# One table replaced: the order of every engine's steps in a fused attention and gated feed-forward kernel

## The chip, the cores and the metric

The kernel runs on one core of a Trainium2 chip. The metric is device time in microseconds (us). The kernel before was timed in three runs: 216.54, 216.66 and 220.53 us, median 216.66. One further execution was recorded by the hardware profiler; its span, from the first to the last instruction, is 213.9 us at a granted TensorE clock of 1.000.

## What is computed

Block-sparse attention for 4 batches of 8 heads, 768 tokens and 64 channels, in blocks of 32 tokens (a row of blocks also sees three sampled ones). The heads' outputs are put side by side (512 channels) and go through a feed-forward layer whose gate is a convolution over three neighbouring tokens.

```python
scores = scale * np.matmul(q, k.transpose(0, 1, 3, 2))
mask = np.abs(blk_i - blk_j) <= window
mask = mask | (blk_i == 0) | (blk_j == 0) | (blk_i == n_blocks - 1) | (blk_j == n_blocks - 1)
...
scores = np.where(mask, scores, -1000000000.0)
attn = np.exp(scores)
attn = attn / (np.sum(attn, axis=-1, keepdims=True) + 1e-09)
return np.matmul(attn, v).astype(np.float32)
...
h = np.maximum(x @ w_in, 0.0)
for k in range(K):
    conv_out += conv_w[k][None, None, :] * hp[:, k:k + S, :]
gate = 1.0 / (1.0 + np.exp(-conv_out))
return (h * gate @ w_out).astype(np.float32)
```

## The kernel before

The program first builds a list of 1758 steps. Each step has a name, the engines that may do it, the steps it needs, and the buffers it takes. A table, ORDER, then says in which order the steps are put down. For each it holds two characters (the step's number to base 64), one letter for the engine where the step has a choice (P TensorE, A ScalarE, V VectorE, G GpSimd, S SyncE), and one character for each buffer that the step is the first to use. put_down reads the table and calls each step's function; that is all the scheduling there is. Every engine then runs its own steps strictly in that order, and waits where an input or a buffer is not ready.

The steps, in the order in which data goes through them:

- Loads. Sixteen pairs of heads (four for each batch) need q, k and v. The first pair comes in float32 by SP and ACT queues. All others are issued by POOL (L239), with conversion to bf16. POOL issues in order, and between the loads stand tiny "pace" copies (L414, L656) that make POOL wait until a given exp, or an earlier load, is done.
- Getting q and k transposed into a slot (tiles e and o, five slots). Pairs 0 to 5: TensorE transposes (L466 for k, L504 for q) into PSUM, copied on by DVE or ACT (L340, L336). Pairs 6 to 15: two DMA transposes issued by SP (L581, stg<-nat), then two DVE copies (L340, e<-stg and o<-stg). Rows 64 to 87 of a slot hold the mask; they are made once (L309, L320 and L322, k rows by L340 or L336) and copied to the other slots (24-row copies). v is copied into its tile beside a column of ones (v_cp: vt<-vn).
- 144 attention units, 18 for each half batch of 384 tokens ("segment"). The last half batch is cut into a segment of 256 and one of 128 tokens, so there are nine, 0 to 8. A unit is two steps of score matmuls on TensorE (L742, st<-e,o; 8 blocks of 128x128, 1024 columns), one exp on ACT (L753, pt<-st), and two steps of matmuls with v (L775, av<-vt,pt). Two PSUM buffers st, two av and two mix; six pt buffers. So the scores of unit u+2 wait for the exp of unit u.
- After the last av step of a pair of heads: reciprocal (L692, rcp) and normalisation (L694, xtok<-av,rcp) on DVE, then a transpose of xtok into xT. In segments 0, 1, 7 and 8 this is done by TensorE (L713) and a copy (x_cp). In segments 2 to 6 it is a DMA transpose issued by SP (L703, xT<-xtok), four for each segment.
- First feed-forward matmuls (L864, mix<-xT,winb), which need all four xT parts of their segment; relu by ACT (L884) or DVE (L886) into hE; three products and two sums for the convolution on DVE (L916, L924), or, for segment 8, matmuls with diagonal matrices (L935); tanh on ACT (L963, L940); plus one (L966) and product (L971, gT<-m,hE) on DVE.
- Second feed-forward matmuls (L802, mix or st<-woutb,gT), four steps of two for each of 24 blocks of 128 tokens; eviction ("ev", o2s<-mix) by ACT (L336) or DVE (L340); store issued by SP (L809).

SP's queue therefore carries, in table order, the L581 and L703 transposes, the stores, and eight small copies of mask rows for the last batch (m_last, o<-mlast and e<-mlast).

The engine is a choice of the table for these steps alone: the casts of the first pair, copies out of PSUM (k_cp, q_cp, x_cp), the two mask copies, v_cp, relu and ev. In the kernel before, DVE does 13 of 16 v_cp, 30 of 64 relu and 11 of 24 ev.

Of the kernel before, what the change touches and what calls it, by code (L numbers as in the profile page):

```python
# [25 lines left out]
6o15yV6p690Z6d6e6q05+16t04v1P05/V6i6j6u6k06y16l6v14w6z160+6m06r06s6A26nV6D00S6E0X4xhW12l06F3hZ00/6I16JhX4y2m6K4
h+hYV06R06Sh/Vi316T5i4ii06W14z176Xik6wi5Ai00iji16Y04A2x11Q1i2V6/0701RAil4B6x2116B7417111SV6C75iq1290im6G762ic1
2aV47d0idir7ein7i14C2bV2z26H7j7f36L6M1is2c04DieV6U6V6Z7k46+7n06N12eV7oit2217p5722dV7s17t24V2n023V7u0737x0iu7y2q1
2oV02B02A7z1777G16O7H784E2pV2F27g0iv7h7L07926P0io4F7l2H37M7I27a7m7q7rip07v7w7A7N37B16QV17Q12rV7R7J0W7K7b07S47V0
7C07W2kV47O2sV7X57D2C4G82183107P7E17T8407cV8707FV887Uiw7Y8918c1ix2J12I7Z8d2yV0i602GV18e28h04H7+12N08i7/i7i918j3  # L30
4Ii8V2f0ia8508m12DV1ibA8nif08o4igiy28u0iz868a8vihAiA2P8z12Q18A8w5iBiO1iG3800iP8B0iC8E02K4J2t18biH8f8FiDiI8J12S8g
8kiJ8l81A8K8piE8q18G18x8yiK2g08CiF8D2RiL8H2iViQ2hV2OA28IiMiU02EViV8L2iN2T0iW2LV2iR2X2Y18R0iSA08SiX8T38W1iYV18X
i+18Y4i/2MV8/090j0Vj109158r2941958sj22Uj71960j3V9909a8Mjm0j409b12+9h1jo2/08t29i8Njnj89j2j58O0jp9m09nj9V8U0j6A8V
319r1jq9o3ja1jbju1jd0jvjrje8P9s9w0jcAjx8Z321308+92jfA93jwjj19t49xjC2jg0jhjyiZ9y5369E1js372jkjiV9798jz9cjE9F2u0jD
9d19G09J0jA9k9KjF9l9L19e19O1jt9p9q339PjlV9u2wA9T02vAjB9U9vk819Q2jK3k9jL9z9V3jGjY0393a29Y19f9A9ZjHjMa409g9H09IjN
9M9+4jZjOa59N9R8QjI9SjP9W3c9XjJa91aaa65kajQiT9/jRj+3bab09B2ae09Cj/2VV3af9Dk0A2kb3h2WVaj1ag1k20a11a2k33d0kcA3k4
2ZA3k5jS1k6V1a30jT34V4akjUal2ar0k1jVa01asjWA0ke0kfat3jXkh1kgV1kiaw135V3kkjAax3l3kn0ay4kokC03i0kk1kEaB0kpAklkDaC
kmAa7kFa8acaG1aD5kq0kGadaHkK1kt1kH3nahkMaL0kr3o13mkLaI0aikuksVamaMkvAkNkz03eaN1aT1kOaUkw1kS2ankPkx3skIkAao0kTaY0
aV2aZkJ1au0avazaAkyVaEkBAaFaJb11kVa+3b2aKkQl61apaOb34b60kRaqb7lc0kUb85be1k+3bfl7l03pbg0aP1kWaWbj0bkaQ2aXk/kXa/b0
b4bo1aRb5b9bl1bal1aSbh0bpldkYl2bq2bt0bikZbubmbb1l3lebcby1bzbv3bdl4bnl8l5brbsbA43qV0bG0bHk7l938V43fV1bI5lf3v3w1  # L40
laV2bL1bMlgA0bwbQ03rVli1bN0lh3gVljll0kdlkV3jA0lm3AbRlblnVbV1bWbS1lr1lG0lo0lIlsbX23x3B1lplHc10c2ltV3t1lqAbxc61lJ
c33c7bBbC1lO1lx1lylKc84cb0bJlzVcclD0lLlQcg1bKlP3ychlu1cd5bD0lRbObPlvbEbTci0lElMcl0bF1lSbUcmlwAbY3KlNct13L0lTlA1
lW2bZculYcn1c40lB3zlXc5c9calFVcv33Hcy03I2czb+2lUcelZlCAmg03PlVcA4cD1cfcEl+mh3Mb/cF2cjcI0ck3uV1ma1c0m23l/cJcom3
cp1cQ1cRcK5m4cw3CcxcBm5cCcGmbcS0m0m6cV0cHcLm1cM3NcWm7c+1cq1micrcX1c/m8mccscN0m9cT0cUd03d30cOd4mjcPd54cY3Zmd3+2
mkV1d81d9meV0mm03Q0da5dg03DV2mn3JV2mo3EV423OcZmfdhd1mpdi03W3Gdl1mqV3dmmy1dn1mz3/mB0mC3X0mAA0dq0mDVd2drms1mW0ds2
mtmX3Rdv1dwmYmudx3mZmE0mv40m+431d6d7mwV2mFm/dD0dbmGVdEdI1dc1n0dF4mH1n10mIdJdd2mJAmN04cde4d3dN0dK5mOn21df2dj41dO
n3dkmK1n4dP0mL494a1n5domxdpdS1dTmPVmMA4hdtdudX0dU13SV3dYdy3TVmQ1mRdZ2n6e314e4i0e4na2dzmT0nbe53mUmSVdG0e80dHe9n7
mVVdLed1dA1eeni3ea4nw1dBdMdQdRncdVef5dCdWd+ei04fndejnq0n8ek0e00eq1neer3Fd/1n9e6e744es1ev0njewnrnkex3eA1e1eb3VeB
ecnlege2nfehel4gem3YV3et0eF0nmeC4nx4ong4p2eueyen2eznheGnneK1eonyeH5eLepnonsnpeDeEeM045V4eS0eT4jnteU2eX1nuV0eYnz
eZ14bV4eI48eJnAV2eNf00mrf1eO1eP1f5146Vf23mlf6nC0eQ47nDf74nI1eR0nEVnJfd04qV0nKAfe4kV1nL0ff5nM3Ufi1nNVnvfjnF14lV  # L50
fk0eV4nnGo60eWnBfn0fonHAo8nR0fp2nSo7fs1n+1e+e/ftnTAn/nO1fu1nPo9fx0o0fyf3nQAf4o1nU0fz3fF1oafGf8f9o2nVfH4nX1oe2fg0
fK0offLo3nYogfhfP1fa0fM5flnZVfQfmfqo4frfbobfU0o5fvfcfVnWAohoA1fR0ocfwou0om3fAodfW2g01g1onfB1fIovoig21g50oog6oBop
ojfJfNfC2fOoqfSg73fTga1fDgbfXfYokfEg30org4g8olg9gj0gkgc4osoCotowgl5fZ1go1f+gpoxgq0f/gdoDoyV3gt0gugeoM0gv24mgf0oN
ggozoOoEA1oPoFgC1oQA0gDgh1gH0giA1gIoS0gE1oToV1oUV1gJ3oWgM1oXVgNp20gO4p3pe1p51pgp6p4Apfgm1gV0p7AgngrphoY0oZpigW
o+Agso/1pu0pjp0pwoG0pvp1Ag+1g/gX5oHpm2oIpnh00oJpogwh30pph4oKA2gxpxpb1h52gF0pqoLpcp80gy2pkoRgGpdAgKgzgLgPhc1prpy
# [962 lines left out]
```

## Time and profile before

| | before |
|---|---|
| median of 3 runs | 216.66 us (216.54 to 220.53) |
| span of the profiled execution | 213.9 us |
| median less that span | 2.74 us |
| TensorE matmul busy (PE) | 203.6 us, 95% |
| TensorE weight load busy (PEld) | 154.0 us, 72% |
| ScalarE busy (ACT) | 193.5 us, 90% |
| VectorE busy (DVE) | 186.6 us, 87% |
| GpSimd busy (POOL) | 60.4 us, 28% |
| DMA moved | 24.81 MB, mean 116 GB/s |

The profile does not give the whole device time of the execution that it shows; what lies around its span is taken to be the 2.74 us by which the median of the runs is longer. Busy times count an instruction from its start to its last write, so consecutive ones overlap: an exp takes 1027 ns, but a line of them starts one every 0.92 us.

### The profile page before, as it was taken

What the parts mean: (1) busy time and instruction counts of PE and PEld (TensorE: products, weight loads), DVE (VectorE), ACT (ScalarE), POOL (GpSimd) and SP (SyncE); (2) the same over time, 40 slices, a digit from 0 to 9 for tenths busy, and PEclk for the clock granted to TensorE, in tenths of its full rate; (3) what the DMA queues carried; (4) which work ended last, traced back from release to release, by engine and by line L of the source; (5) the groups of instructions that cost most, each with busy time, mean ns of one, the idle gap of its engine ahead of it and who ended that gap; (6) DMA issues with size and microseconds to landing.
All of it is one profiled execution on the core that took longest, in us unless ns stands there. A gap on an engine that the chain in (4) does not pass through costs nothing.

```text
span 213.9 us, 6829 instructions
## 1 busy us (share of the span) xinstructions
PE 203.6 (95%) x2702; PEld 154.0 (72%) x2721; DVE 186.6 (87%) x577; ACT 193.5 (90%) x252; POOL 60.4 (28%) x117
## 2 busy tenths in 40 slices
PE   7899999999999999999999999999998999999991
PEld 3679978887677775778776766787786867785740
DVE  4899989999989994999999978999799939999980
ACT  6999999999899997999999977999999988997642
POOL 8883455733323130500327152730000000000000
PEclk9999999999999999999999999999999999999999
DMA  6999898998888977693599869699941130200205
GB/s 181 186 195 202 132 123 119 113 172 99 99 123 99 138 133 162 122 106 74 103 234 96 116 104 188 105 143 114 134 154 23 20 122 3 98 5 21 80 0 196
DMA packets 48935, 24.81 MB, mean 116 GB/s; under 512 B 35120, under 2 KB 45832, under 8 KB 48904
## 3 DMA queue, kind: packets, MB, share of 16 engines
q0 software_dynamic: 19728, 11.05, 43.0%
q1 hardware_dynamic: 28888, 13.05, 30.0%
q8 instruction: 21, 0.34, 0.7%
q10 hardware_dynamic: 288, 0.30, 0.4%
q14 instruction: 10, 0.08, 0.1%
HBM read 23.08 MB, written 6.29 MB: 137 GB/s over the span
## 4 chain that ended last, share of the span: by engine, by line
PE 66%; DVE 24%; ACT 6%; issue 3%; ACTq 0%; DVEq 0%
PE st L742 19%; PE mix L802 16%; PE mix L864 12%; PE av L775 10%; DVE m L916 9%; ACT pt L753 4%; DVE m L924 4%; DVE hE L886 3%; PE st L802 2%; PE mix L504 2%; PE av L230 2%; DVE xtok L694 1%; DVE gT L971 1%; DVE o L340 1%; DVE e L340 1%
## 5 line engine op out<-in xcount | busy, mean ns | idle before, releaser
L753 ACT ACTIVATE pt<-st 128x1024 bf16<-128x1024 f32 x144 | 141.3, 1027 | 5.6 <-PE st L742 4.2
L775 PE MATMUL av<-vt,pt 128*128 128x65 bf16 x1152 | 60.4, 193 | 0.2
L775 PEld LDWEIGHTS <-pt 128*128 128x128 bf16 x1152 | 52.3, 97 | 10.1
L864 PE MATMUL mix<-xT,winb 128*128 128x384 bf16 (+2 forms) x288 | 52.8, 308 | 0.3 <-DVE hE L886 0.3
L916 DVE TENSOR_SCALAR m<-hE,cw 128x382 bf16<-128x382 bf16 (+2 forms) x192 | 49.4, 320 | 0.2
L802 PE MATMUL mix<-woutb,gT 128*128 128x512 bf16 x157 | 44.6, 379 | 1.6 <-DVE gT L971 0.6
L742 PE MATMUL st<-o 88*128 88x128 bf16 (+1 forms) x240 | 44.5, 229 | 0.3 <-ACT pt L753 0.2
L742 PE MATMUL st<-o,e 88*128 88x128 bf16 (+1 forms) x228 | 44.2, 233 | 0.2 <-ACT pt L753 0.2
L742 PE MATMUL st<-e,o 88*128 88x128 bf16 (+1 forms) x224 | 42.5, 234 | 1.2 <-ACT pt L753 1.1
L742 PE MATMUL st<-e 88*128 88x128 bf16 (+1 forms) x208 | 41.8, 239 | 0.4 <-ACT pt L753 0.2
L742 PEld LDWEIGHTS <-o 88*128 88x128 bf16 x464 | 34.3, 97 | 8.9 <-issue 2.0
L742 PEld LDWEIGHTS <-e 88*128 88x128 bf16 x436 | 32.9, 97 | 9.0 <-issue 0.9
L924 DVE TENSOR_TENSOR m<-m 128x764 bf16<-128x764 bf16 (+2 forms) x64 | 33.8, 533 | 0.3
L864 PEld LDWEIGHTS <-winb 128*128 128x128 bf16 x288 | 24.2, 97 | 8.2 <-issue 0.8
L963 ACT ACTIVATE m<-m 128x764 bf16<-128x764 bf16 (+2 forms) x32 | 26.3, 821 | 1.9 <-DVE m L924 1.8
L414 POOL COPY pace<-pt 1x1 bf16<-1x1 bf16 x24 | 7.6, 315 | 58.9 <-ACT pt L753 58.8
L802 PEld LDWEIGHTS <-gT 128*128 128x128 bf16 x192 | 15.7, 97 | 11.7 <-DVE gT L971 2.3
L886 DVE TENSOR_SCALAR hE<-mix 128x384 bf16<-128x384 f32 (+2 forms) x30 | 16.4, 553 | 7.9 <-PE mix L864 7.6
L884 ACT ACTIVATE hE<-mix 128x384 bf16<-128x384 f32 (+2 forms) x34 | 16.5, 492 | 3.1 <-PE mix L864 2.2
L971 DVE TENSOR_TENSOR gT<-m,hE 128x764 bf16<-128x764 bf16 (+3 forms) x36 | 18.3, 511 | 0.5
L694 DVE TENSOR_TENSOR xtok<-av,rcp 128x384 bf16<-128x384 f32 (+2 forms) x36 | 18.2, 507 | 0.4
L239 POOL DMA_DIRECT2D nat<-in_q_dram x23 | 16.9, 734 | 2.4 <-issue 1.9
(88 smaller groups left out, 170.0 us busy)
## 6 DMA issues: line engine op xcount, KB each, us to landing
out_dram<-o2s SPq DMA_DIRECT2D x24, 256.0 KB, 2.6
nat<-in_k_dram POOLq DMA_DIRECT2D x15, 192.0 KB, 4.0
vn<-in_v_dram POOLq DMA_DIRECT2D x15, 192.0 KB, 5.5
nat<-in_q_dram POOLq DMA_DIRECT2D x6, 192.0 KB, 4.2
winb<-in_moe_w_in_dram POOLq DMA_DIRECT2D x2, 512.0 KB, 8.4
woutb<-in_moe_w_out_dram POOLq DMA_DIRECT2D x4, 256.0 KB, 4.8
nat<-in_q_dram POOLq DMA_DIRECT2D x9, 96.0 KB, 5.4
nq<-in_q_dram POOLq DMA_DIRECT2D x6, 96.0 KB, 4.5
```

The source lines that it names most:

```text
L239: return op(name, {eng: occ}, lambda e: on(e).dma_start(out=dst(), in_=src), prio, deps, dma=(kind, service), **kw)
L694: nm = op("norm", {"DVE": t_dps(128 * C)}, lambda e: nc.vector.tensor_tensor(out=xtok_t[xk.index][:, 0:C].rearrange("p c h d -> p h c d"), ...
L742: nc.tensor.matmul(out=st[:, 128 * x:128 * (x + n_)], lhsT=QK[kc % 2][s][0:88, 1, hh, kc // 2, :], rhs=QK[par][s][0:88, 0, hh, idx:idx + n ...
L753: nc.scalar.activation(out=pt_t[ptb.index], in_=st_t[stb.index], func=AF.Exp, bias=0.0, scale=0.125)
L775: nc.tensor.matmul(out=o[:, off:off + 65], lhsT=pt_t[ptb.index][:, 128 * x:128 * x + 128], rhs=V_t[vslot_b[P].index][:, hh, kc, 0:65], sta ...
L802: nc.tensor.matmul(out=acc(), lhsT=gT_t[gb.index][:, ffc, 128 * t:128 * t + 128], rhs=woutb[:, ffc, :], start=(ffc == 0), stop=(ffc == NFF ...
L864: nc.tensor.matmul(out=mix_t[hb.index][:, w1 * y:w1 * y + w1], lhsT=winb[:, fc, 128 * ffc:128 * ffc + 128], rhs=xT_t[xt_buf[n].index][:, f ...
L886: nc.vector.tensor_scalar(out=dst, in0=src, scalar1=0.5, scalar2=0.0, op0=ALU.mult, op1=ALU.max)
L916: nc.vector.tensor_scalar(out=m_t[cb.index][:, x, y, 0:w], in0=hE_t[heb.index][:, f0 + y, t0 + x:t0 + x + w], scalar1=cw[:, x, f0 + y:f0 + ...
L924: nc.vector.tensor_tensor(out=m[:, a_, :, 0:w], in0=m[:, a_, :, 0:w], in1=m[:, b_, :, 0:w], op=ALU.add)
L963: th = [op("tanh", {"ACT": t_act(2 * w) + 0.04}, lambda e, cb=cb, w=w: nc.scalar.activation(out=m_t[cb.index][:, 0, :, 0:w], in_=m_t[cb.in ...
L971: nc.vector.tensor_tensor(out=gT_t[gtb.index][:, f0:f0 + 2, t0:t1], in0=m_t[cb.index][:, 0, :, 0:w], in1=hE_t[heb.index][:, f0:f0 + 2, 1 + ...
```

## The change

The table ORDER is replaced as a whole. The list of steps, what each does and needs, the tiles and their numbers are the same; 1758 steps are put down in both. A few of its 40 lines, from the start and the end:

```diff
 ORDER = """
-000m010g0f0n0h02030410o0i0t050p0j0q0s060zA1t00k0r070AA0l081u18A1090v1F00a0b1aA0c1H20d0N0w01bA19V1c00O0xA1i11f0
-1dV00yA0e1jV1l11eV1kA1gA0R1o00E4K11hA4L0D4P01nA1mV1B14Q4M01v10u0Q0P1I1wV14R14U11xV4V1T11y00G4W24Z01V34+1zV0F1AA
...
-pUA1hKqvpXpVqihL1hQhRpYAhMVpPhS0hx1hThyAq60qjhU0q01hVVq7qR0qSq8q1qTAq9qkq2AqO0qaqPqlr31qbqX1qQVqYr4qcq+0qZAqU0qd
...
-rrrkqHrsA1rlrtrmA3rn
+0g0m000102030n0o0p0q1t00410506070t0zV0f1u1F01H10i0s0u0Q0T0S1o01B10h0r0v18A21aA0AA1bV0j19A08090a0b0c0d1c00w00P
+1dV01eA0xV1i10e1l01f11kA0yA1jV1nA1hA1I1T11V31W2521gV1mV0D0O0E0G2724r0k0l4K14L4M04P04Q1v01y11wV11zV1xV0R0F0N4R1
...
+rjqKqAqBqLqMA3qNrbrcrkrlrqrrrmA2rsA1rnrtqEqFqGA0qH
 """
```

Read as steps, it moves these from engine to engine:

| step | ACT before, after | DVE before, after |
|---|---|---|
| cast of k, first pair | 2, 1 | 0, 1 |
| cast of q, first pair | 1, 2 | 1, 0 |
| mask rows of k, first slot | 2, 1 | 0, 1 |
| mask rows of q, first slot | 2, 1 | 0, 1 |
| q_cp, 64x512 | 2, 0 | 9, 11 |
| q_cp, 64x256 in two heads | 3, 2 | 8, 9 |
| v_cp, 128x768 | 3, 1 | 13, 15 |
| relu, 128x384 | 28, 27 | 28, 29 |
| x_cp, 128x128 | 2, 3 | 2, 1 |
| ev, 128x512 | 13, 15 | 11, 9 |

TensorE's, POOL's and SP's steps stay on their engines and change places among themselves. The order changes that the prediction speaks of:

- ACT, start. Before: both mask copies, cast q, cast k, cast k, mask q rows (two), then copies out of PSUM, then the first exp. After: cast q, cast k, one mask copy, cast q, then copies and the other mask rows.
- TensorE, start. Before: the mask matmuls (L309) come ahead of the first k transposes (L466). After: behind them.
- SP. The four xT transposes of segment 4 stood last as third, fourth; now fourth, third. Those of segment 6 likewise. Transposes of pair 15's q (L581) now stand ahead of the last xT transpose of segment 5.
- POOL. The q load of pair 8, which stood behind the pace copy on exp 42, stands behind the one on exp 48; smaller moves of the same kind follow for pairs 9 to 14.
- TensorE, end. The last eight steps are of L802, for the last four blocks of tokens, 20 to 23. Before, by block: 20, 21, 21, 20, 23, 23, 22, 22. After: 21, 21, 22, 22, 23, 23, 20, 20. Block 20's eviction is on DVE before, on ACT after.

More of the change, by code (lines that the diff above doesn't have):

```diff
@@ L20 @@
 ORDER = """
-000m010g0f0n0h02030410o0i0t050p0j0q0s060zA1t00k0r070AA0l081u18A1090v1F00a0b1aA0c1H20d0N0w01bA19V1c00O0xA1i11f0
-1dV00yA0e1jV1l11eV1kA1gA0R1o00E4K11hA4L0D4P01nA1mV1B14Q4M01v10u0Q0P1I1wV14R14U11xV4V1T11y00G4W24Z01V34+1zV0F1AA
-1W5214/30H532521p11sV05445b02715c1qV1C00I1rA4N0125g15d55h1DV4O4S1J14r1GV1281EV5i04T4X1KV25l05m134Y1LV1M05n15q14s
-1NV5r1450511OV555s25610K5z05A5e0J5f5j5B35E15705F1UV20U14t1X0582j05G45J00V5K1YV31+15L51ZV5k5o5O15P1/V5p5t20V5u5Q0
-5T00T5v15U26V35C05D5w5H5V16010Y614u5I155M115N6225R6500M660B05S6730C6a16b0L5W5X1636c4646f05Y26g5Z591685x06h55aV0
@@ L26 @@
[L26 to L55, printed above, removed]
@@ L56 @@
-hdgQpl1gY1gZhe1h1p9psh2gR1h6ptgA1hh0paAh7gShigBAhq1h80pC3hrhj3pK0pDgT1pLh9hs4gUVhf0hz0pFhgha1hkpzhl1hbVhApEhthu
-pZ1hB5hv2pGp+hwhE1pHp/VhFhN0hC1hOpAhG0q31pIpBq4pJhDpMq5Aqe1hHpNhP2hJ1hm0pQ1qfhnpRpOA3qhpSqu2ho0qgpThpA2qwhI0pW0
-pUA1hKqvpXpVqihL1hQhRpYAhMVpPhS0hx1hThyAq60qjhU0q01hVVq7qR0qSq8q1qTAq9qkq2AqO0qaqPqlr31qbqX1qQVqYr4qcq+0qZAqU0qd
-qVq/qm3qC1qWAqor01qDqnr50qI0r1r6r80r2rd1qpri0qqr9rer7ro1qrqxrprf1qyra0qJqsqzqtrjqEqAqBqKrbqLrcrgqFrhqMA2rqqGV0qN
-rrrkqHrsA1rlrtrmA3rn
+0g0m000102030n0o0p0q1t00410506070t0zV0f1u1F01H10i0s0u0Q0T0S1o01B10h0r0v18A21aA0AA1bV0j19A08090a0b0c0d1c00w00P
@@ new lines @@
+1dV01eA0xV1i10e1l01f11kA0yA1jV1nA1hA1I1T11V31W2521gV1mV0D0O0E0G2724r0k0l4K14L4M04P04Q1v01y11wV11zV1xV0R0F0N4R1
+4U14V4Z04+4W21AV1p0521531C14/35b05c5445d51sV00I4N04O4S4T1qV1GV11rV1DV0H1EV5g15h4X1J05i05l05m5n11M15q15r124Y5051
+555s21KV21LV13281OV1NV5z05A5615e5f5j5E15F5k1X05B35G45J04s144t2j04u154v1P04w164x2l04y2m4z175K1+15O15P1UV20K0J5o
+5L55Q01YV31ZV20V5701/V5826V35p5t5T05U0M0B05u5C00U10V0C5v10/5w0X5V1601615D5H5910Y5aV0650666225I5M5N6735R6a16b5S
+5W5X1636c46f06g5Y210646h5685x05yV0+5Z6o16p696d6e6q06t06u6i6j5+16k06l6y16z6r06s6m06v15/A6w6D06E6A26F36nVhZ1hW0hX
@@ new lines @@
+h+6I16J6R06x0ZhYV0h/Aii0ij6K46B6S1Q01RVi016W16X6T56Ci11SV6/070ikil4A2x14B2114C2z14D2A4E2F24Fimi30i4i2Vi5Viq1ir
+it6Y07116G6H6L6M1741752917d07eis6N12aV42bViuin7627f3ic0id6U6V7i16Z6O7j6+72737n0777o2c1ieA7k42eV2dV7p57s17t787g0
+7h2n02217u07l792io0W23V24A7m7q7x07y7G17r7H7a2oV02pViv2q17z12sV2rV7v7b07L07M7w6P17A7B10L7I27N36QV1iw7Q17Ri617J
+7S47V07W7Ki77X52kV47C07Dip07cV821837O7P7T7E0870887U7Y7Z8408c18di8Vix117+27/2yV0891i91ia8e28h08i8j37FVif08m1ig
+8508nibViy2iziBihA868a8o48u08biG3iA8v8f8018g8k8l8z18A81ViC8w5iHiJiI8B0iDiO08piP8E08q12H34G2I4H2N04I2f04J8x8F8y
@@ new lines @@
+iKiEiF8C8J12B02J12CiL2K8K2P2g12iA8D2hV2Q22t12S8L18G2iMiNiQ2DV12EViU1iViWiXiYA08R18SiR8r12LV22MV2GV1iSV18s8W0i+1
+8Xi/8T3j0V2OV28Y48/190j10j2j3V9159408H8I959602+2R2/0j419919a9b28Mj58Nj70j89h0jm0jnjpjojqj6A8U08Vj9Vju1jwjv8O0jr
+8Z9i9m1jxjy9j38+9njd1je929o4jfAja08Pjz939r02T09sjb979w19x989c9d1jcV9e2jC2jAjEjB2u12vVjs9f9kjg0jh9t59y08t2321jiA
+9E09l9F2X2Y12U319p9q9u9J19G18Q9Kjj0jk9L29v9z9O09P9AjlA2wVjtjDjFjGjK3jLjNjMiT9T19H09IjO9UjY19M9N9Q39R9SjZ9V4jH
+9Y09Za41k809+0jPjI9W9Xa5jJ9B19C9g9Dk9a90aaka9/jQjRa0130363937233a65ab1j+j/kbae1a72VV3k0A2kcA3afag2a8aj0ke1akkf
@@ new lines @@
+ackgV1a10adahkh0kikjVkC0ar1askDa2kFal3at4aw0axkk1kn0aiamankoay5aB1klaCaG0kpAkmAaD2k1kt0au0aHkq1krkuavaL1aI32ZV3
+ao2aMazaAaEaFaJaT0aUkEkGkK1kLkN2WVapa303k3a13l3kM3cksAkz1aN03nkvAiZ3d0aqaKaOaV4kHkO34V4aP1k20aQ1aY1kAk3k4aZ3b3h
+3i03m3skS2kU35VkIkPb10k5b2kBVa+5kw1b32kxb61aWaXa/b0k6A1b7b81be0bf3o1aRaS3pkQkTkVkyVk+3k/jS0jTkJ1kRkWl0l1bg3b4
+bj1bkjUb5bo0bpjVb9lc1kd3ebl0jWV2l2bq4kXkYldbt1bubabb0bcbv53t1by0bh0l60bibmbdl3kZbzbnbG1bHjX3qV038V4l73jV0l4l5
+bA2lel8bL0lfl9bI1bMbQ1lgA0ll1bRlm3uV13rVbN3laV3li0ljlnAbS0brbV0bWbs3v3w23A3xbX4lr1ls3fV13gV3yc11c2bwbxbBlkVltA
@@ new lines @@
+lo0lG0lHlIlJlKlpc35lLc60lu1lqVlO1lPlQlRlSbC1c7cb1c82bD2ccbJbKbObPbTbUbYbZbEcg0chlvlx0lwVlycd1cl1lMlblzVlW2lXlN
+b+1b/lYci3lTcmct0cuc40c5lD1c9lA0calhcn0cv5cy1czcA2lBcecfcjckcD0lEcocEcI1cJlCAlFAcF1cp1cw3K3zma0cxcBlZlUlVcCl+cG
+mb3B1bF13Cc0cQ0cRcHl/3L03P3Q0m23m3m0m5m4cK3mg1cV1cLcWcMm6m1cq0cN2cOcS0m7m8m9crmhcPc+0mic/mccT1cX5cUd023M3Nd31d4
+d53mdmjd80d9da0mkA2meV3cYcZd1csdg1d2d6d7dh3Z3+3my0mz3H3I2mB13O423/di4mf3RmCdl0dmmAV0mDAdq1mW03DV2dn5drmm0dbdd1
+dedc0mH1dv0mIds2mJA403W3X0djdwdx3dD1dEmE1mFmnmomYmXmZm+mGV3EVdF0m/mpmqA04c4d1dI0dkdJn0dK1dN1dOdP4mK1mLmN0mOdodp
@@ new lines @@
+mPAn21n4mMAn3n53SV3n6dtdudydS0dTdX1dzdYdG1dHmT0mU3JV2dA2na2dB3TV3V41494a14hncn7dU5dLmQ1dMdQdRe30dVmRdZ2e4e81dW
+d+mSVnbe9df23U3YV3n8mVAe53ea0ms0mted0ee4e4f4gmuei1eje00n10ndnee1n9nw1ef1mrni3nknjek4d/0e6mvmwV3eq0e7ebeceregeh
+nfngnhelemev1ewes5nxex3eA0eBeC0nq0nreF1eGet1eueK0eLnseyen1dC431nlnmnnml4i03Gnyeoe2ezeH1eM44445V44jnonpnznAA0eS1
+ntep46VeT4kV1eX0eYnuV24bV44o4p24qA04lVnI1nJnKVnL0nMnNVo60eU2eZ5f01f1f23o7o9eDeEnC1eIf50f6eJeNo8oaeP2f70fd1feff1
+nDnF0nEVnGnHVn+1n/o1o0obfi0fjeO0o2eVnR1eWnSfn1fk4foe+e/f3f4fp2fs0ftfu5nTVocnO0nPnQVeQ474n4m48nBnvo3fx1fyf8f9fa0
@@ new lines @@
+fbeR0fcnU1fF0nVfg1fGfhflfz3fmfqfrfH0o4o5odfK1fLnX0nYoe2ogoffM1fvfP0fQfwnWAfR4fA3Fk7nZVohoifC1fU1fVou1ovfW2g00fD
+om3onopoooqg1g25ojfB0oA0g51oBg6g73okolorga0gbfIfJfNfOfSfTfXfYg31g4g8gj1gc0gkfZ2f+osotoCowg9go0oxgdgegpoDgl1gt1
+guoyV0f/fEoEV2oM1oNoOoPgm0gv4oV0gC1oWoQV1gq2ozoS1oToUV1oXApe0oFoRgf0ggpgpfphgDgE5p50p6p21p3gH0gImxp7Ap4Apu1pign
+gM1gNgJ3gO0pvgrgsgwgxpxgy2oY0pjgV0gF1gGgWo/1oZo+Ap0p1VgzgKgLg+1pwpkpm2popl1pyg/pb0p81gPp9gX1h02h30gQh4hc1gY0gZ
+paAgh1hdh1pch2h54h6gR1pngSgiA1h7gA1hh0hipdAgBVoG0oHhe5pphj3hf1gT1gUAoIoJpqh80h9ha1hgprpC3pEhbVhkpDhm2hnhq1hrpF
@@ L61 @@
+pZ1p+p/VoKA0hs0ho0hz0hpA2hl0hApzpspGhB1q30q4htpW1pXhE1q5ApHpAqe0qfqhptqgqipBpIpYAhFhG2huhC1hN0pK0pLpQ1pJhOhDhP4
+hHhJ1pMpNpOA2hv0hKhwq62q7q8qu1q9pRpShL0pThI1hQqjhMAhRpUA1hS2hThx0hU1hVVqvqaqxhyAqkqwq00qR1qSqTAq1q2AqO1qPr30r4
+qQVpPqbqcqdqlr53qX0qYqm0r6r7qnqU1q+1qVqZAqWAq/r02rd0qC0qI1rer81qDr9qoqpr1r2qqqJrf3ro0rpqypVoLqrqzra2rgrhqsqtri1
+rjqKqAqBqLqMA3qNrbrcrkrlrqrrrmA2rsA1rnrtqEqFqGA0qH
 """
```

## Prediction

> **What bounds the kernel now.** I read the page's first two parts, then the busy time by stretch, then who waited for whom, then the chain of work.
>
> ```profile
> PE 203.6 (95%) x2702; PEld 154.0 (72%) x2721; DVE 186.6 (87%) x577; ACT 193.5 (90%) x252; POOL 60.4 (28%) x117
> PE   7899999999999999999999999999998999999991
> ACT  6999999999899997999999977999999988997642
> ```
>
> TensorE is above nine tenths in nearly every slice; ACT is too, with dips. By stretch (busy us of PE, PEld, DVE, ACT, POOL; then clock, DMA share and GB/s):
>
> ```profile
> 8.00:20.00 12.00, 10.89 (x172) 8.95 (x170) 11.31 (x29) 11.76 (x14) 7.53 (x13) 1.00 1.32 195
> 20.00:60.00 40.00, 39.49 (x618) 32.37 (x618) 36.00 (x120) 38.63 (x46) 18.79 (x38) 1.00 1.00 126
> 60.00:100.00 40.00, 39.31 (x507) 29.34 (x509) 36.04 (x107) 38.52 (x51) 8.74 (x17) 1.00 0.80 122
> 100.00:140.00 40.00, 39.42 (x494) 29.15 (x496) 36.97 (x101) 36.98 (x45) 17.11 (x31) 1.00 0.85 134
> 140.00:180.00 40.00, 38.85 (x551) 30.18 (x555) 34.80 (x101) 38.26 (x49) 0.99 (x3) 1.00 0.61 90
> ```
>
> From 20 to 180 us TensorE is idle for 0.51 + 0.69 + 0.58 + 1.15 = 2.9 us in all. From 8 to 20 us DVE (0.69 idle) and ACT (0.24) are fuller than TensorE (1.11). What TensorE waited for (us in all, times, longest):
>
> ```profile
> PE st L742 <- ACT pt L753: 1.7, 6, 0.7
> PE st L802 <- ACT o2s L336: 0.7, 1, 0.7
> PE mix L802 <- DVE gT L971: 0.6, 2, 0.3
> PE mix L864 <- DVE hE L886: 0.3, 1, 0.3
> ```
>
> How much of the busy time is work? Rows of the chain that run without a gap give the packed rate: a unit's scores 0.445 us (L742 x6), 16 av matmuls 0.49, four L864 0.65, eight L802 1.73, six transposes 0.45. With the page's counts: 144 x 0.445 = 64.1; 72 x 0.49 = 35.3; L864 56 x 0.65 and the two narrow forms 5.4, 41.8; 24 x 1.73 = 41.5; transposes 18 x 0.45 = 8.1; warm-up and the rest about 8. That is 199 of the 209.0 us from the first matmul (1.27) to the last (210.28). So no order can give back more than about 10 us, and both orders have these 199 us to do.
>
> **What moves between engines.** By the mean durations of the rows, ACT gives up a k cast 0.51, a mask copy 0.70, mask q rows 0.47, q_cp 2 x 0.57 + 0.37, a relu 0.49 and two v_cp of 0.86: 5.4. It takes a q cast 0.35, two ev of 0.59 and an x_cp 0.27: 1.8. Net -3.6 us. DVE takes the same work at its own prices (v_cp 0.35, q_cp 0.41 and 0.27, relu 0.55, mask rows 0.55 and 0.57, k cast about 0.43, half again its 0.26 for half the width): 3.9, and gives up 0.26 + 2 x 0.69 + 0.23 = 1.9. Net +2.0 us. As TensorE's work is unchanged, both count only where TensorE waits for them.
>
> **Start.** These rows are DVE's, from the timeline.
>
> ```profile
> 5.97 0.57 DVE L340 COPY e<-mix 64x384 bf16<-64x384 bf16 x2 [0.30 <-PE mix L466]
> 10.17 0.42 DVE L340 COPY e<-mix 64x512 bf16<-64x512 bf16 x1
> 10.62 1.09 DVE L340 COPY e<-e 24x1536 bf16<-24x1536 bf16 x2
> ```
>
> Before, ACT does two mask copies (2.95 to 4.29) ahead of the casts, and the first k transposes stand behind the mask matmuls at 4.79; DVE gets k at 5.97. The k load had landed at 3.68. After, the casts come first and k_tr precedes the mask matmuls, so DVE has k when its own cast ends: a4 ends 4.60, cast 0.43, so about 5.1. The first scores still wait for ACT's copies behind the second q load (landed 5.35), about 6.7 for 6.82. The first exp then follows two copies instead of three, about 7.3 for 7.88, and two copies that stood among the first five exps (0.27 us each by start-to-start) are gone. On DVE the 24-row copy that the second pair's scores wait for (first of the two in the row at 10.62) ends near 10.4 instead of 11.25: 0.8 earlier start, constants moved ahead, less 0.2 for a q_cp that came over. Bounds: 0 if the second k load is what is late, -1.4 if DVE and ACT gains add. I take -0.9, the DVE reading, since that row ends last.
>
> **Middle.** Adding up ACT's steps in both orders at their start-to-start rates (exp 0.92, relu 0.39, tanh 0.73), ACT has 4.9 us less ahead of exp 84 than before (3.6 moved, the rest comes later in the order), while TensorE's work in front of each unit is within 1 us, save near unit 66. TensorE's waits for ACT shrink: 1.7 less 0.74 in the start leaves 1.0 that the view shows, and 2.9 is all its idle time. Bounds 0 and -2.9; I take -1.4, half, nearer to the 1.0 shown.
>
> **SP's transposes.** Here a cover gets thinner.
>
> ```profile
> DMA to landing us min/median/max: 2.3/3.9/6.0
> 98.87 4.26 SPq L703 DMA_TRANSPOSE xT<-xtok  x2
> ```
>
> In segments 2 to 6 the first L864 needs the last xT part. Between the segment's last av and that L864 TensorE had, at the packed rates, 9.2, 5.2, 6.5, 6.0 and 6.5 us of other work before; it has 7.3, 4.6, 4.9, 6.1 and 5.6 after. The path is: DVE's queue until rcp (1.4, 1.4, 1.1, 1.7 us before in segments 3 to 6), rcp 0.19, norm 0.56, SP's issue, landing. For segment 3 the last issue was at 101.23 and L864 ran at 104.37 without a gap, so landing took 3.1 us at most. With 3.1: segment 3, 0.95 + 1.2 + 3.1 = 5.25 against 4.6, 0.65 late. Segment 4, whose third norm now comes behind a g1 and a g2 (0.27 + 0.47), 5.75 against 4.9, 0.85. Segment 6, where one 1.2 us issue now stands behind another, 6.25 against 5.6, 0.65. Segments 2 and 5: 0. Sum 2.15; I take +2.0. With 2.3 it is 0; with the median 3.9, 0.25 + 1.45 + 1.65 + 0.2 + 1.45 = 5.0. I take 3.1 because it is the one of these five places that the trace bounds.
>
> **POOL's loads.** Pair 8's q load now waits for exp 48 (about 62 us) instead of 42 (52.5): issue 0.72, landing 5.4, so about 68.5, transposed by about 76. Its copies run on DVE from 79 on (e<-stg). Cover 3 us; if it went, DVE would stand still with everything behind it. The others of this kind have as much. Cost 0, upper bound 1.
>
> **End.** After the last transposes the set of steps is the same. Before, the last product on DVE ends at 207.47 and three L802 steps follow, the last held 0.72 us by an eviction of the same PSUM tile: 2.8 us. After, six steps follow the last product, 6 x 0.43 + 0.45 = 3.05, with that eviction no longer ahead; DVE has one sum (0.42) fewer in this stretch. 3.05 - 2.8 - 0.42 = -0.2 (bounds -0.9 and +1.0, if the two gains or the three steps come alone).
>
> **Sum.** -0.9 - 1.4 + 2.0 + 0 - 0.2 = -0.5 on a span of 213.9: 213.4. With the 2.74 us by which the median exceeds that span, 216.1.
>
> **A rule that speaks for more, one that speaks against.** The Trainium skill (Perfetto Trace Analysis, Identifying the Most-Contended Engine) holds matmul busy time for a bad measure and asks for the weight-load share: here 72%, against 95%. By it TensorE has room and ACT would be the bound, so that ACT's 3.6 us come out in full (third rival below). The packed rates above, 199 of 209 us, bear it out for a part only. The Trainium skill (SBUF — State Buffer, SBUF: two separate sides) says that a VectorE copy in a two-port mode locks GpSimd out of SBUF, so that it cannot write descriptors. The trace does not show it: POOL's load issues stay at 0.70 to 0.83 us while DVE is nine tenths busy.
>
> **Rivals.**
> 1. Transposes land late (slower). One mechanism: the last xT part of a segment, on SP. At the median 3.9 us the sum is -0.9 - 1.4 + 5.0 - 0.2 = +2.5, time 219.1. It decides from 3.25 us on. For it: the median; a landing of 6.0 us among the five whose end is told. Against: 3.1 in segment 3.
> 2. DVE becomes the bound (slower): no middle gain, its 2.0 us on the path: -0.9 + 2.0 + 2.0 - 0.2 = +2.9, time 219.5. For it: 36.97 of 40 busy between 100 and 140, and a chain that gives DVE 24%. Against: it still idles 3 to 5 us in each such stretch.
> 3. ACT was the bound: -0.9 - 3.6 - 0.2 = -4.7, transposes hidden, time 211.9. For it: ACT's 1.4 us of idleness from 20 to 60. Against: TensorE's 0.5.
> 4. The new order is no different where it counts: 216.7, within my own case.
>
> **How the numbers follow.** Forecast (with 4) 0.45; rival 1 0.24, 2 0.19, 3 0.12. The forecast's own range is 214.3 to 218.3. For 8 in 10 I go to 212.6, which leaves out most of rival 3, and to 220.2, which takes in 1 and 2 at their prices; no more than 2 in 10 is left. A difference of 2% (4.3 us: below 212.3, above 221.0) is about the least that a measurement of this kernel can tell from no change. Faster than that is most of rival 3, 0.09; slower is the upper part of 1 and 2, 0.11; within, 0.80.
>
> **What would show it.** First exp near 7.3 and the tenth near 16.3 (now 17.24); ACT busy near 190, DVE near 188.5; TensorE gaps ahead of L864 near 104, 126 and 175 us; none ahead of L742 for pair 8; a last L802 without a wait for o2s. Wrong if TensorE's idle time grows by over 3 us, or falls by 3, between 20 and 180.

## The result and the profile after

The changed kernel took 222.46, 223.07, 224.88 and 225.91 us, median 223.97, beside 218.19 for the kernel before (its three runs and a fourth of 219.73). The ratio is 1.033, 95% interval 1.026 to 1.041: slower, and above the predicted range. Both kernels now and then run about 2% slower with the same steps; the ratios here compare undisturbed executions only and so differ from quotients of medians. The profiled execution has a span of 220.4 us, 6.5 more than before. These are its busy times and two rows of its slices.

```profile
PE 204.6 (93%) x2703; PEld 153.9 (70%) x2721; DVE 191.9 (87%) x582; ACT 190.7 (87%) x247; POOL 58.4 (26%) x117
PE   7889999999999999999999899898998999999992
ACT  5889999999789998989899899898999859998532
```

ACT has 2.8 us less work and stands still for 29.7 us in place of 20.4. DVE has 5.3 more. The same stretches as before (PE, PEld, DVE, ACT, POOL; clock, DMA share, GB/s):

```profile
8.00:20.00 12.00, 9.89 (x158) 8.46 (x158) 10.77 (x29) 10.24 (x11) 7.44 (x13) 1.00 1.33 199
20.00:60.00 40.00, 39.21 (x616) 32.26 (x616) 37.01 (x119) 37.80 (x46) 16.21 (x35) 1.00 0.93 116
60.00:100.00 40.00, 38.55 (x499) 29.00 (x502) 36.46 (x106) 36.98 (x48) 10.41 (x21) 1.00 0.82 116
100.00:140.00 40.00, 38.44 (x501) 28.77 (x504) 35.86 (x96) 36.70 (x46) 14.70 (x29) 1.00 0.87 128
140.00:180.00 40.00, 36.93 (x495) 27.61 (x499) 35.85 (x98) 35.37 (x41) 2.40 (x4) 1.00 0.51 95
```

TensorE's idle time is 2.1 us from 8 to 20 (1.1 before) and 0.8 + 1.5 + 1.6 + 3.1 = 6.9 from 20 to 180 (2.9 before). With half a microsecond more behind 180 that is 5.5 of the 6.5 us; the other 1.0 is in its busy time. No stretch holds the loss alone. What TensorE waited for (us in all, times, longest):

```profile
PE mix L802 <- DVE gT L971: 2.2, 5, 1.0
PE st L742 <- ACT pt L753: 1.6, 3, 0.7
...
PE st L742 <- DMA o<-mlast: 1.0, 1, 1.0
PE mix L504 <- DMA nq<-in_q_dram: 0.9, 1, 0.9
PE mix L466 <- DMA nat<-in_k_dram: 0.7, 1, 0.7
...
```

What ACT waited for, in the kernel before and then in the changed one:

```profile
ACT pt L753 <- PE st L742: 4.2, 10, 1.0
...
ACT m L963 <- DVE m L924: 1.8, 3, 1.4
```

```profile
ACT pt L753 <- PE st L742: 7.0, 13, 1.4
...
ACT m L963 <- DVE m L924: 5.3, 9, 1.2
```

TensorE's waits for ACT are what they were (1.7 before). Those for the products of DVE have grown (0.6 before), and those for transfers are new (2.6 us in all, none before). ACT in its turn waits 7.0 us for scores (4.2 before) and 5.3 for DVE's sums (1.8 before). The chain that ended last, in the kernel before and then in the changed one, by engine:

```profile
PE 66%; DVE 24%; ACT 6%; issue 3%; ACTq 0%; DVEq 0%
```

```profile
DVE 51%; DMA 18%; PE 16%; issue 7%; ACT 4%; POOL 2%; ACTq 0%; POOLq 0%; DVEq 0%; SPq 0%
```

A chain that was mostly TensorE's now goes through DVE and through transfers. One of its transfers, in the changed kernel's chain from 91 us on:

```profile
91.36 8.93 DMA nat<-in_q_dram
100.29 0.02 issue
100.31 3.27 DMA stg<-nat
...
103.67 0.55 DVE e L340
104.22 0.54 DVE vt L340 x2
104.76 0.28 DVE m L966
105.03 0.02 issue
105.06 0.57 DVE gT L971
105.63 0.05 issue
105.68 1.04 PE mix L802 x4
```

The q load of pair 11 takes 8.93 us to land. In the view of its tile, for the loads that POOL issues (least, median, most):

```profile
DMA to landing us min/median/max: 2.5/4.2/8.9
```

POOL issues it 4.5 us behind the k load of pair 10 (86.89), with pair 11's k, pair 10's q and a v load between; before, pair 10's k and q were issued at 74.73 and 77.28, 11 to 13 us ahead of pair 11's. SP's transpose of it follows at once, DVE stands still for 0.36 us until the transposed tile is there, and the product for L802 stands behind that copy in DVE's queue: TensorE idles 0.50 us. A load is paid for by TensorE through three queues.

### The profile page after: what moved, and what is told of

It is laid out like the page before. It is cut to its first block, busy times and chain, and to the rows that moved or that the text cites. A ratio compares the mean times of both kernels' runs of the same rounds, so it can differ in the third digit from the quotient of the medians.

```text
span 220.4 us, 6822 instructions
## 1 busy us (share of the span) xinstructions
PE 204.6 (93%) x2703; PEld 153.9 (70%) x2721; DVE 191.9 (87%) x582; ACT 190.7 (87%) x247; POOL 58.4 (26%) x117
## 4 chain that ended last, share of the span: by engine, by line
DVE 51%; DMA 18%; PE 16%; issue 7%; ACT 4%; POOL 2%; ACTq 0%; POOLq 0%; DVEq 0%; SPq 0%
DVE m L916 13%; DVE m L924 9%; DMA nat<-in_q_dram 6%; DMA stg<-nat 5%; DVE gT L971 5%; DVE xtok L694 5%; PE st L742 4%; DMA vn<-in_v_dram 4%; DVE hE L886 4%; PE mix L864 4%; PE mix L802 3%; DMA nat<-in_k_dram 3%; DVE e L340 3%; DVE m L966 3%; ACT pt L753 3%
## 5 line engine op out<-in xcount | busy, mean ns | idle before, releaser
L775 PE MATMUL av<-vt,pt 128*128 128x65 bf16 x1152 | 58.3, 193 | 0.6 <-DVE xtok L694 0.3
L775 PEld LDWEIGHTS <-pt 128*128 128x128 bf16 x1152 | 51.0, 97 | 10.3 <-issue 0.7
L864 PE MATMUL mix<-xT,winb 128*128 128x384 bf16 (+2 forms) x288 | 53.6, 308 | 0.6 <-DVE hE L886 0.4
L916 DVE TENSOR_SCALAR m<-hE,cw 128x382 bf16<-128x382 bf16 (+2 forms) x192 | 50.3, 319 | 0.6 <-ACT hE L884 0.3
L802 PE MATMUL mix<-woutb,gT 128*128 128x512 bf16 x158 | 44.8, 379 | 3.4 <-DVE gT L971 2.2
L742 PE MATMUL st<-o,e 88*128 88x128 bf16 (+1 forms) x228 | 43.1, 233 | 2.1 <-DMA o<-mlast 1.0
L742 PE MATMUL st<-e 88*128 88x128 bf16 (+1 forms) x208 | 41.1, 239 | 0.9 <-ACT pt L753 0.7
L864 PEld LDWEIGHTS <-winb 128*128 128x128 bf16 x288 | 24.2, 97 | 7.9 <-issue 1.0
L802 PEld LDWEIGHTS <-gT 128*128 128x128 bf16 x192 | 15.8, 97 | 15.4 <-DVE gT L971 6.3
L886 DVE TENSOR_SCALAR hE<-mix 128x384 bf16<-128x384 f32 (+2 forms) x31 | 16.9, 552 | 7.1 <-PE mix L864 7.0
L414 POOL COPY pace<-pt 1x1 bf16<-1x1 bf16 x24 | 5.7, 237 | 61.9 <-ACT pt L753 61.9
L694 DVE TENSOR_TENSOR xtok<-av,rcp 128x384 bf16<-128x384 f32 (+2 forms) x36 | 18.2, 508 | 0.6
L971 DVE TENSOR_TENSOR gT<-m,hE 128x764 bf16<-128x764 bf16 (+3 forms) x36 | 18.1, 511 | 0.7
L884 ACT ACTIVATE hE<-mix 128x384 bf16<-128x384 f32 (+2 forms) x33 | 16.0, 499 | 2.5 <-PE mix L864 2.3
```

What stands on the lines that cost most here:

```text
L694: nm = op("norm", {"DVE": t_dps(128 * C)}, lambda e: nc.vector.tensor_tensor(out=xtok_t[xk.index][:, 0:C].rearrange("p c h d -> p h c d"), ...
L742: nc.tensor.matmul(out=st[:, 128 * x:128 * (x + n_)], lhsT=QK[kc % 2][s][0:88, 1, hh, kc // 2, :], rhs=QK[par][s][0:88, 0, hh, idx:idx + n ...
L775: nc.tensor.matmul(out=o[:, off:off + 65], lhsT=pt_t[ptb.index][:, 128 * x:128 * x + 128], rhs=V_t[vslot_b[P].index][:, hh, kc, 0:65], sta ...
L802: nc.tensor.matmul(out=acc(), lhsT=gT_t[gb.index][:, ffc, 128 * t:128 * t + 128], rhs=woutb[:, ffc, :], start=(ffc == 0), stop=(ffc == NFF ...
L864: nc.tensor.matmul(out=mix_t[hb.index][:, w1 * y:w1 * y + w1], lhsT=winb[:, fc, 128 * ffc:128 * ffc + 128], rhs=xT_t[xt_buf[n].index][:, f ...
L886: nc.vector.tensor_scalar(out=dst, in0=src, scalar1=0.5, scalar2=0.0, op0=ALU.mult, op1=ALU.max)
```

## The experiments

Unless something is said to be left out, each kernel computes all. Ratios are to the kernel before, with their 95% intervals; the changed kernel stands at 1.033. In the short diffs, steps are numbered by kind (mul and add are the convolution's products and sums, rcp and norm L692 and L694, diag the diagonal matrices, s a step of scores, q_tr a transpose of q by TensorE, xb L581, x_xb L703, out a store; the rest as above).

**Dependent neighbours on DVE.** DVE's 5.3 us where 2.0 were expected led to the first theory, D. In the timeline of the changed kernel, an instruction that does not read its predecessor's result starts before that one has ended; one that does read it starts behind its end:

```profile
101.80 0.34 DVE L966 TENSOR_SCALAR m<-m 128x764 bf16<-128x764 bf16 x1
102.07 0.18 DVE L692 RECIPROCAL rcp<-av 128x6 f32<-128x6 f32 x1
...
104.68 0.34 DVE L966 TENSOR_SCALAR m<-m 128x764 bf16<-128x764 bf16 x1
105.06 0.56 DVE L971 TENSOR_TENSOR gT<-m,hE 128x764 bf16<-128x764 bf16 x1
```

The first pair overlaps by 0.07 us; the second leaves 0.04 between them, since L971 reads what L966 writes. Over the whole trace the difference in starts is 0.116 us. The old table has 40 such pairs, the new one 89. The rival, W, is waits for loads, transposes and evictions. Four kernels were run.

Run 1, the new table with the pairs taken apart (89 to 3):

```diff
 DVE, new table
-norm2 rcp3 norm3 x_cp3 diag3 relu0
+rcp3 norm2 norm3 x_cp3 relu0 diag3
...
-mul4 add2 mul5
+mul4 mul5 add2
```

> The new table, with VectorE's steps alone exchanged with a neighbour or the next but one, so that only 3 of its instructions follow the one that they read from directly, instead of 89. Theory D (dependent neighbours): in both profiles a VectorE instruction starts 82 ns before the end of an independent one ahead of it, but 34 ns after the end of one that it reads from, so each such pair costs 0.116 us. 86 pairs less are 10 us of VectorE time; VectorE carries half of the chain that ended last, so 4 to 8 us come back: ratio to the kernel before 0.995 to 1.015, VectorE busy near 182 us instead of 191.9. Theory W (waits on loads, SP's transposes and evictions, set by the other engines' order): those are untouched, the ratio stays at 1.03, within 1 us of the new kernel.

Measured: 228.97 us, 1.046 (1.035 to 1.056). DVE's busy time fell by 4.1 us, less than half of what D has, and the time rose, outside both expectations:

```profile
PE 204.1 (91%) x2703; PEld 153.8 (69%) x2721; DVE 187.8 (84%) x582; ACT 191.2 (85%) x247; POOL 58.6 (26%) x117
```

Run 2, the old table with pairs brought together (40 to 89):

```diff
 DVE, old table
-rcp0 v_cp2 norm0
+rcp0 norm0 v_cp2
...
-mul1 relu2 add0
+mul1 add0 relu2
```

> The old table, with VectorE's steps exchanged with their neighbours so that 89 instructions follow the one that they read from, as in the new table, instead of 40; all other engines as before. Theory D: 49 x 0.116 = 5.7 us more VectorE time; 3 to 6 us on the end, ratio 1.014 to 1.028. Theory W: none of the waits it names is made, ratio 1.00, at most 1 us more from steps that come one place later.

Measured: 221.69 us, 1.018 (1.010 to 1.026), as D has it; but see run 5.

Run 3, the old table with its pairs taken apart (40 to 2):

```diff
 DVE, old table
-rcp2 norm2 x_cp0
+rcp2 x_cp0 norm2
...
-rcp7 norm7 relu4
+rcp7 relu4 norm7
```

> The old table, with 38 of its 40 dependent neighbours on VectorE put apart in the same way. Theory D: 4.4 us less VectorE time, of which 1 to 3 us reach the end since TensorE is 95% busy: ratio 0.985 to 0.995, faster than both kernels. Theory W: ratio 1.00.

Measured: 226.13 us, 1.031 (1.022 to 1.040): slower where D has it faster.

Run 4, one of W's waits taken away: the transposes that waited 0.9 us for a q load.

```diff
 TensorE, new table
-s7 q_tr2 s8 s9
+s7 s8 s9 q_tr2
```

> The new table, with the one TensorE step that transposes the first pair's second half of q moved back behind the next unit's scores, where it stood in the old table. The gap of 0.91 us that TensorE has there (its load lands at 11.49 us) goes. Theory W: 0.9 us of the 1.5 us by which unit 20 is late come back and stay to the end: ratio lower by 0.004. Theory D: VectorE carries the chain soon after, so under 0.4 us is left of it at the end.

Measured: 224.77 us, 1.035 (1.030 to 1.040). The wait for nq is gone from the view and the time is no shorter; those for exps and for mask rows are 0.4 and 0.5 us longer in its profile. The 0.004 that W expects is less than these intervals can tell. D falls with runs 1 and 3. The pairs explain part of DVE's busy time, not the kernel's.

**Is it any exchange?** Theory L, formed here: a step that comes one place later makes another engine wait, wherever it is, because the queues of the three engines fit each other closely. Run 5 is the control for the first three.

```diff
 DVE, old table
-mul0 mul2 mul1
+mul0 mul1 mul2
...
-q_cp17 q_cp16 add3
+q_cp17 add3 q_cp16
```

> The old table with 38 exchanges of two neighbours on DVE that do not depend on each other, spread over the whole run at random; the number of instructions that directly follow the one they read from stays at 40. If dependent neighbours are what costs time (theory D), nothing changes: ratio 0.995 to 1.005. If the old table is fitted so closely that any DVE step that comes one place (about 0.3 to 0.5 us) later makes TensorE or ACT wait (theory L, formed after the two runs in which pairs were taken apart became slower), the ratio is 1.01 to 1.03, as in those runs.

Measured: 221.32 us, 1.020 (1.013 to 1.027). These 38 exchanges, which leave the count at 40, cost as much as the 38 of run 2, on average about 0.11 us each; run 2 therefore says nothing for D.

**Engines or order?** Runs 6 to 8 take the change's parts one at a time.

```diff
 run 6: old order, new engines (57 steps)
-relu3 ACT, v_cp7 ACT, ev1 DVE
+relu3 DVE, v_cp7 DVE, ev1 ACT
 run 7: new order, old engines
-relu3 DVE, v_cp7 DVE, ev1 ACT
+relu3 ACT, v_cp7 ACT, ev1 DVE
 run 8: new table, old order on SP and POOL alone
-SP: x_xb0 xb6 xb5 x_xb1 out0 x_xb2 x_xb3 xb7
+SP: xb5 x_xb0 xb6 out1 xb7 x_xb2 x_xb1 out0
```

> All steps in the old order; the 57 steps whose engine differs go to the engine that the new table gives them, at their old places. Rival 2 of the prediction (load moved to DVE): DVE busy 188.5 or more, ratio 1.01 to 1.02, and most of the loss is here. Theory L: also slower, 1.01 to 1.03, but with waits at the places where copies and relus changed engine. If the order carries the loss and the engines do not: 0.995 to 1.005.

> All steps in the new order; the 57 steps stay on the engine of the old table. DVE busy about 2 us less than in the changed kernel. Rival 2 (load): most of the loss gone, ratio 1.00 to 1.01. Order carries it: 1.02 to 1.035. Theory L: 1.03 or more, since the new order was not made for these engines.

> The new table on TensorE, DVE and ACT, with the old order of SP's and POOL's queues (transfers, loads, masks). The theory of transfers (loads at 8.7 and 11.5 us, the last mask behind two transposes at 171 us, transposes of x): 1.5 to 3 us come back, ratio 1.015 to 1.027. If what DVE and ACT do in between carries the loss: at most 0.7 us, ratio 1.028 to 1.04.

Measured: run 6 226.55 us, 1.044 (1.038 to 1.051); run 7 246.53 us, 1.138 (1.131 to 1.145); run 8 254.07 us, 1.169 (1.158 to 1.180). The new engines in the old order cost about as much as the whole change, the new order with the old engines four times as much. Runs 6 and 8 lie above all that was expected of them; run 7 lies where theory L has it. Not all of this is waiting. The granted clock was 0.59 between 8 and 20 us in run 6's profile, 0.91 from 100 to 180 in run 7's and 0.74 from 100 to 140 in run 8's, where the kernels before and after show 1.00; and TensorE's busy time is 216 and 218 us in runs 7 and 8, against 205 to 207 in runs 13 to 15 below. In run 7 the largest of TensorE's waits is for ACT, in run 8 for DVE's products, and there DVE itself waits for transposed tiles:

```profile
PE st L742 <- ACT pt L753: 9.9, 12, 2.4
```

```profile
DVE e L340 <- DMA stg<-nat: 14.4, 3, 7.0
PE mix L802 <- DVE gT L971: 13.5, 7, 7.2
```

So the new table's engines, order and transfers fit each other. How much of its loss is the engines' or SP's and POOL's cannot be read from changing those alone. Run 8 also corrects W: giving the transfers their old order does not give the loss back.

**Which engine bounds either order?** Runs 9 to 12, 17 and 18 shorten one engine's work and leave every step at its place. What they leave out: columns from 192 on of each convolution group's second sum (DVE), one product of four in every second wide L864 group (TensorE), columns from 256 on of 28 tanh (ACT).

```diff
 runs 9 (old table) and 10 (new table)
+h = w if b_ == 0 else min(w, 192)
-nc.vector.tensor_tensor(out=m[:, a_, :, 0:w], in0=m[:, a_, :, 0:w], in1=m[:, b_, :, 0:w],
+nc.vector.tensor_tensor(out=m[:, a_, :, 0:h], in0=m[:, a_, :, 0:h], in1=m[:, b_, :, 0:h],
 runs 11 (old) and 12 (new)
-todo = [(fg, 0, fc) for fc in (2 * part, 2 * part + 1)]
+todo = [(fg, 0, fc) for fc in (2 * part, 2 * part + 1) if not (fg % 2 and fc == 1)]
 runs 17 (old) and 18 (new)
-th = [op("tanh", {"ACT": t_act(2 * w) + 0.04}, lambda e, cb=cb, w=w: nc.scalar.activation(
+th = [op("tanh", {"ACT": t_act(2 * w) + 0.04}, lambda e, cb=cb, w=min(w, 256): nc.scalar.activation(
```

> The old table; the second sum of each convolution group on DVE covers 192 of its 256 to 386 columns only (the rest of the second sum is left out), 32 instructions, about 6 us less DVE work by the rows of 0.55 us for 764 and 0.29 us for 260 elements. If TensorE bounds the old order and DVE has room (the prediction's reading): at most 1.5 us come out, ratio 0.993 to 1.0. If DVE is on the path of the old order as well: 3 us or more, ratio below 0.987.

> The new table with the same shortened sums (same part left out). If DVE bounds the new order (rival 2, and the share of 51% in its chain): 4 us or more come out of 223, ratio to the old kernel 1.005 to 1.015. If the new order loses time in many small waits of all kinds without one bound: about 1.5 to 2.5 us come out, ratio 1.02 to 1.027.

> The old table; TensorE leaves out one of four L864 products in every second group of the wide form (28 matmuls of 0.163 us, 4.6 us, that part of the first product is left out). If TensorE bounds the old order: 3 to 4.6 us come out, ratio 0.979 to 0.986. If ACT or DVE hold it as much: under 2 us, 0.991 or more.

> The new table with the same products left out. If TensorE still bounds the new order, as much comes out as of the old one. If DVE (or ACT) has become its bound: under 1.5 us, ratio to the old kernel 1.026 or more.

> The old table; 28 of the tanh steps on ACT cover 256 of their 382 or 386 columns (the rest of the tanh is left out), about 28 x 0.22 = 6.2 us less ACT work by the rows of 0.85 us for 764 and 0.63 us for 512 elements. If ACT bounds the old order (rival 3): 4 us or more come out, ratio 0.982 or less. If no engine bounds it alone, as the shortened DVE and TensorE work suggest: 1 to 2 us, 0.990 to 0.996.

> The new table with the same shortened tanh. ACT has 2.8 us less work here. If ACT is the new order's bound: 4 us or more come out of 223, ratio to the old kernel 1.01 or less. If no engine bounds it alone: 1 to 2 us, 1.02 to 1.028.

| work shortened on | old table: ratio | comes out | new table: ratio | comes out |
|---|---|---|---|---|
| DVE (busy 4.1 and 4.0 us less) | 0.991 (0.986 to 0.995) | 2.0 us | 1.019 (1.011 to 1.026) | 3.2 us |
| TensorE (28 x 0.163 = 4.6 us) | 0.992 (0.987 to 0.997) | 1.8 us | 1.026 (1.014 to 1.038) | 1.5 us |
| ACT (busy 3.5 and 4.8 us less) | 1.001 (0.995 to 1.007) | none | 1.028 (1.022 to 1.034) | 1.1 us |

What comes out is the ratio's distance from 1, or from 1.0332, times 216.7; in the old column it is good to about 1.2 us, in the new one to 2 or 3, so that there only DVE's is more than its uncertainty. Runs 9 and 10 lie between their two expectations, run 17 outside both. In the old order 4.6 us less of TensorE's work bring 1.8 (0.6 to 2.9), and 3.5 us less of ACT's bring nothing: neither alone bounds it. One reservation: a shorter step also moves every release behind it, and run 5 shows what such moves can cost, so a small gain can hide a larger one that was lost again. In the new order DVE's work comes out most, which agrees with its 51% of the chain; that it does so more than in the old order is not shown.

**Where along the run?** Splices: the first steps of one table, the remaining ones in the other's order, with buffer numbers given out anew. They are cut where the two tables have done nearly the same steps, at unit 22 (28 us) and unit 75 (101 us).

```diff
 runs 13 (n = 265) and 15 (n = 872); runs 14 and 16 with old and new exchanged
-order = new
+order = old[:n] + [step for step in new if step not in old[:n]]
```

> The old table's first 265 steps (to unit 22, about 28 us) and then the remaining steps in the new order, with the new engines. By the traces the new order has lost 1.5 us of its 6.5 there. If the start's loss is one that stays (the forecast's first term, with the wrong sign): ratio 1.02 to 1.026. If the start's loss is made up later or the rest has its own: 1.03 or more.

> The reverse: the new table's first 265 steps, then the old order. If the start's loss stays: ratio 1.005 to 1.01. If it is absorbed: 1.00. If a junction between two tables costs as much as the changes themselves: above 1.015.

> The old table up to unit 75 (872 of 1758 steps, about 101 us), the new order behind it. By the traces 2.4 of the 6.5 us are lost before and about 4 behind that point. If the loss is spread over the whole new order and adds up: ratio 1.016 to 1.022. If it comes from the start or the first half: 1.01 or less.

> The new table up to unit 75, the old order behind it. If the loss is spread and adds up: ratio 1.01 to 1.014, and with the run before it the two losses sum to the whole 3.3%. If a fault of a later place carries it: 1.005 or less.

Measured: run 13 224.68 us, 1.039 (1.029 to 1.048); run 14 219.62 us, 1.014 (1.006 to 1.022); run 15 223.18 us, 1.030 (1.027 to 1.033); run 16 220.95 us, 1.022 (1.012 to 1.031). Run 14 lies between its expectations, runs 15 and 16 above theirs. Every piece of the new order costs something: its first eighth 1.4%, its first half 2.2%, its second half 3.0%. The two halves sum to 5.1%, the pieces at unit 22 to 5.3%, and the whole costs 3.3%: the costs do not add up. Either the pieces share one loss, or a joint of two tables costs something by itself, as a few dozen exchanges do.

The starts of the exps in the traces, held against the kernel before, tell more. In run 14 they are 2.2 us late at unit 20, 2.4 at unit 60, 2.5 at unit 125 and 3.0 at the last: up to there the old order neither makes a delay up nor adds to it, and this joint costs next to nothing. In run 15 they are 1.0 us late at units 9 to 75 (for a late k load, as told below) and 7.2 at the last unit: behind an old first half the new second half loses 6.2 us, nearly as much as the whole change, whose last exp is 6.5 late. How much of the 6.2 is this joint's is not told. Replacing the new start by the old one brings nothing back: run 13 is on time at unit 20 and 7.5 us late at the last one.

## Why the prediction was wrong

**The bound.** The failed step is the first: that TensorE, with 199 of 209 us of packed work, bounds the old order, so that only its visible gaps and five named places count, and every other place stands at nothing. In its stead the changed kernel shows 2.6 us of waits for transfers (none before) and 2.2 for DVE's products (0.6 before), 4.2 of the 5.5 us of new idle time, at places that the sum put at nothing or at a gain. Between 20 and 180 us TensorE's idle time grew by 4.0 us, past the 3 that the prediction itself named as the sign of being wrong. Run 5 shows the same fault without the change: 38 exchanges on DVE alone, none of which such a sum would price, cost 2.0% (1.3 to 2.7). And the bound is not TensorE's alone: run 11 takes 4.6 us of its work away and gets 1.8 (0.6 to 2.9) back, and run 17 takes 3.5 us of ACT's away and gets none. These runs fit a reading in which the old order's gaps are small because three queues release each other just in time, not because one of them has no room; no run shows that directly.

**The engines.** ACT lost 2.8 us of busy time (3.6 forecast). DVE gained 5.3 (2.0 forecast): the moved copies were priced, the 49 new dependent pairs were not. Run 2 shows what they are worth: 49 more pairs on the old table raise DVE's busy time from 186.6 to 191.5, while the exchanges of run 5 leave it at 186.9. Run 1, with DVE at 187.8 and a longer time, shows that the kernel's time did not hang on it alone.

**Start, forecast -0.9.** The first exp came at 7.79 (7.88 before, forecast 7.3) and the tenth at 18.48 (17.24 before, forecast 16.3); TensorE idled 1.0 us more between 8 and 20. The working priced casts and copies; a late load it took as a reason to gain nothing, not to lose. The k load that TensorE waited 0.7 us for was issued at 2.18 in both kernels and landed at 8.62 in place of 7.24. Run 15, with the old start, waits 1.4 us for that same load, so this one is not the order's doing. The wait for the second q load, 0.9 us, comes with the earlier place of its transposes; run 4 moves them back and is no faster, though 0.9 us is less than it can tell.

**Middle, forecast -1.4.** ACT was relieved, but the waits for it stayed at 1.6 us (1.7 before), while ACT's own waits for scores and sums grew by 2.8 + 3.5 us. The relief turned into ACT's idle time. Run 17 had no gain from ACT's relief even in the old order.

**SP's transposes, forecast +2.0.** They cost nothing: no L864 waits for xT. (Its totals of 5.25, 5.75 and 6.25 cannot all be redone from the parts that it lists.) The cover was counted in packed TensorE work, while TensorE came late itself; that this is why they were hidden was not tested. The one wait that the view now shows ahead of L864 is 0.4 us for a DVE relu. Rival 1 falls with it.

**POOL's loads, forecast 0, at most 1.** The working followed pair 8 (its tile came in time, as forecast, though the 5.4 us of landing is the page's row for loads of 96 KB; pair 8's has 192 KB and a row of 4.2) and said that the others have as much cover. They had not: DVE stood twice before a transposed tile, 1.0 us in all, and both times a product for L802 behind it kept TensorE idle, 0.50 us at 105.7 and 0.97 at 153.9. The last mask rows of SP's queue, which the working did not price, held the scores for 1.0 us at 171.2. They are those of pair 12, with which the last half batch opens. Their copy is the first of the four into o in the old order and the last in the new one, behind two L703 transposes. In the kernel before and then in the changed one:

```profile
143.64 0.84 SPq L239 DMA_DIRECT2D o<-mlast  x1
```

```profile
169.08 0.84 SPq L239 DMA_DIRECT2D o<-mlast  x1
```

That this wait comes with the new order is seen in the runs that end by the new table (1, 4, 10, 12, 13, 15, 18): each has it, at 0.5 to 1.5 us, while no run that ends by the old one does. Runs 7 and 8 wait elsewhere. Putting these rows first, and nothing else, was not tried.

**End, forecast -0.2.** The wait for o2s went, as forecast. TensorE's idle time behind 180 us still grew by 0.5, with 0.5 ahead of the last transposes of xtok (0.3 before).

**Rivals.** Rival 2 had the right sign, and a chain with 51% of DVE and run 10 speak for its engine; its price (219.5) left out the dependent pairs and the transfers, and run 1 speaks against DVE's work as the sole cause. Rival 3 falls by runs 17 and 18. The Trainium skill (Perfetto Trace Analysis, Identifying the Most-Contended Engine) has one improve the engine of the highest occupancy first, with TensorE judged by the share of its peak that it reaches and by its weight loads. With weight loads at 72% that is ACT in the old order, at 90%, and run 17 does not agree, since 3.5 us less of ACT's busy time gave nothing. What stays open is what each of the new waits is worth at the end: each was read from one profile, and the two whose removal was tried (run 4's, and W's transfers in run 8) did not show their time given back.
